# A long convolution and a linear attention in one kernel: start-up constants in 16 bits, nine warm-up matmuls, and another order of the units

## The chip, the cores and the metric

The kernel runs on one core of a Trainium2 chip. A core has five engines that each work through their own list of instructions in order: TensorE (PE, with its weight loads shown apart as PEld), VectorE (DVE), ScalarE (ACT), GpSimd (POOL) and SyncE (SP), which here issues all the DMA transfers. An instruction waits until the results and buffers it needs are there, and everything behind it on its engine waits with it. The metric is the time of one execution on the device in microseconds, median over repeated runs.

## The reference

Two independent computations on sequences of 2048 tokens with 576 features share one output, side by side. All inputs and outputs are bfloat16.

```python
# part A: causal short filter on k, product with v, long convolution by FFT, gate with q
k_shift = sum(k_pad[:, t:t + S, :] * shift_k[:, 3 - t] for t in range(4))
kv = k_shift * v
y = irfft(rfft(pad(kv)) * rfft(pad(ssm_k)))[:S] + kv * ssm_D
a = q * y
# part B: linear attention with 32 heads of 18, phi(t) = where(t > 0, t + 1, exp(t)) + 1e-6
q, k, v = split_heads(x @ wqkv)
pq, pk = phi(q), phi(k)
kv = einsum("bhsd,bhse->bhde", pk, v);  z = pk.sum(tokens)
o = einsum("bhqd,bhde->bhqe", pq, kv) / (einsum("bhqd,bhd->bhq", pq, z) + 1e-6)
b = o @ wo
out = concat([a, b], -1)
```

## The kernel before

The whole program is one list of some 295 units, the string `ORDER`. Each entry names a function of the kernel, its arguments, and behind the slash the buffer slots that it takes (four PSUM slots, and named rings in SBUF). The units are recorded in that order, so for every engine the list is also the order of its instructions; no scheduler moves anything. The digits behind the slash decide which earlier unit a new one has to wait for.

Part A works on five chunks `ci` of up to 128 features. The long convolution is a transform by matmuls in two steps of lengths 128 and 16. For the filter (`h`) and the signal (`u`) of each chunk, `h1`/`u1` multiply with the matrices G (128 positions by 128 frequencies for each of 16 residues, real and imaginary part, `s_ps`, L532), an eviction writes `Ch` or `Cu`, a transposing DMA (`ht`, `ut`, L539) makes `Cth` or `Ctu`, and `h2`/`u2` (L555) do the length-16 step into `T` and `SU`. The products `pX`, `pT`, `pS`, `pA` (L567 to L572) run on VectorE or GpSimd. `i1` (L589) and `i2` (L602 to L604) invert the transform; the last step multiplies with q in place, and `st` stores three groups of columns. `cv` (L487 to L493) is the short filter, on VectorE for the greater part, and needs k (`kl`), v (`vl`) and the shift weights `Wj`, which a matmul of ones with one row broadcasts over the partitions (`W_ps`, L387). `hd` and `hT` load D into the filter's first element and turn the filter to position-major by 16 TensorE transposes (L511).

Part B: `xl` loads four blocks of x, `xd` transposes them (L337, L342), `k`, `q` and `qt` are the projections (L451, L460, L468) with phi as an exponential on ACT (L443) and a max on VectorE (L444). `G` multiplies x with phi(k) (L659), `zs` sums phi(k) over the tokens, `kv` and `M` fold wv and wo into one matrix per head block, `den` makes the denominators and their reciprocals, `bc` and `bt` broadcast those and scale phi(q), and `o` and `ol` (L768 to L805) are the output matmuls, with their evictions into `ob` (L299 on ACT, L301 on VectorE) and their stores.

The start-up makes its constants itself. `io` and `ix` compute for each of 16 x 128 positions an integer phase modulo 8192: a float product, converted to 32-bit integers (L145), masked (L146), and for the cosine a quarter turn added and masked again (L150, L151), each in two halves `h`. `sin` turns the phases into G on ACT (L222). `wu` issues warm-up matmuls on zeros (L80), `dc` turns D into a column (`D_ps`, L430). The one row of shift weights lies in partition 96 of a tile whose other 96 rows are zeroed on ACT (`lz`, L377), so that `W_ps` multiplies 97 rows.

On SP, the load of the third filter chunk (`hl.2`) reuses a ring slot and waits for TensorE to have read the slot's content.

Of the kernel before, what the change touches and what calls it, by code (L numbers as in the profile page):

```python
# [8 lines left out]
FP32 = mybir.dt.float32  # L9
# [8 lines left out]
D = 576  # L18
# [19 lines left out]
k.15/3 u1.0.1.0.A/2 hT.2.D/21 u1.0.0.1.A/0 u1.0.0.0.A/3 ht.1.1/0 cv.1.1.DD xd.1.T/1 k.13/2 h2.1.1.1.A/11 cv.1.2.DD
h2.1.1.0.A/0 q.3.1/3 h2.0.0.1.A/21 h2.0.0.0.A/2 ut.0.0/0 cv.1.3.DDP hl.3/0 q.3.0/0 q.1.0/1 u2.0.0.0.A/03 k.6/2
ut.0.1/1 k.7/0 u2.0.0.1.A/3 pX.0.0.D/0 qt.1/1 u2.0.1.0.A/12 u2.0.1.1.D/0 k.5/3 u1.1.1.0.A/12 kl.1 pT.0.0.D k.12/1  # L40
pX.0.1.D/1 u1.1.0.1.A/0 k.14/2 u1.1.1.1.A/3 ht.1.0/0 ql.0/1 cv.2.0.D u1.1.0.0.A/0 pT.0.1.D k.4/1 cv.2.1.DD
h1.2.1.1.A/03 pS.0.1.D pA.0.0.P ut.1.1/1 h1.2.1.0.A/2 hd.3 pA.0.1.D q.1.1/0 h2.1.0.0.A/33 h2.1.0.1.A/2 G.1/10
# [31 lines left out]
def _warm(tc, psum, K, n):  # L74
# [4 lines left out]
    for _ in range({'A': 5, 'B': 8, 'C': 7, 'D': 6}[n]):  # L79
        nc.tensor.matmul(ps[:], lhsT=zero, rhs=zero.unsqueeze(1).to_broadcast([128, 4, 128]), start=True, stop=True)  # L80
# [163 lines left out]
def kernel(  # L244
# [71 lines left out]
    xT = {}  # L316
# [572 lines left out]
```

## Time and profile before

| what | value |
|---|---|
| median of 3 runs | 161.7 us (161.61 to 161.87) |
| span of the profiled execution, first to last instruction | 159.3 us |
| PE busy | 147.6 us, 1966 matmuls |
| VectorE busy | 139.8 us |
| ACT busy | 128.4 us |
| POOL busy | 65.2 us |
| DMA | 31.92 MB, 200 GB/s on average |

The page gives no other time of the profiled execution than its span; the median of the timed runs lies 2.4 us over it. In the profile's rows "L444 DVE ... out<-in ... x16 | 11.8, 751 | 2.7 <-ACT pk L443 2.6" means: line 444, on VectorE, 16 instructions, 11.8 us busy, 751 ns each, and 2.7 us of idle time before them, mostly ended by ACT. In the timeline a row begins with the start and the duration in us, and merges neighbours of one kind ("x16"); such a merged duration runs to the end of the last one. Matmuls overlap each other, so their count times the mean of one is more than the stretch they occupy; the chain of waits gives the stretches without that overlap. Some matmuls are missing from the records (1966 of 1982 weight loads).

### The profile page before, as it was taken

The numbers are of one execution on the slowest core, as the hardware profiler recorded it, in microseconds if no ns is written. First come the engines' busy times: TensorE is split into PE (matmuls) and PEld (weight loads), VectorE is DVE, ScalarE is ACT, GpSimd is POOL, SyncE is SP. The second block draws the span as 40 slices with busy tenths as digits, with TensorE's granted clock in tenths as the row PEclk, the third lists the DMA queues.
The fourth block names the chain that finished last, engine by engine and source line by source line (L and its number), as shares of the span: only waits on it lengthen the run. The fifth ranks groups of instructions, "written<-read, shape, count | busy, mean of one in ns | idle before, by whom it ended". The sixth has DMA issues, their size and how long they took to land.

```text
span 159.3 us, 4563 instructions
## 1 busy us (share of the span) xinstructions
PE 147.6 (93%) x1966; PEld 92.2 (58%) x1982; DVE 139.8 (88%) x170; ACT 128.4 (81%) x157; POOL 65.2 (41%) x67
## 2 busy tenths in 40 slices
PE   6799999999999999999998999999878999998990
PEld 1498564465734467467466568576445565677550
DVE  7978699899899999999899989998999999998420
ACT  7979996899997999959996956997999685786331
POOL 7407541806510970008100019589997077400000
PEclk9999999999999999999999999999999999999999
DMA  3999999990979999999999999684999999444282
GB/s 105 352 368 294 255 239 305 152 231 3 164 130 228 243 228 240 189 212 312 159 196 272 242 155 212 187 141 90 268 152 184 175 324 204 124 117 136 62 264 100
DMA packets 74171, 31.92 MB, mean 200 GB/s; under 512 B 52074, under 2 KB 73509, under 8 KB 74150
## 3 DMA queue, kind: packets, MB, share of 16 engines
q1 hardware_dynamic: 74150, 31.62, 91.7%
q8 instruction: 15, 0.25, 0.7%
q14 instruction: 6, 0.05, 0.1%
HBM read 14.97 MB, written 4.72 MB: 124 GB/s over the span
## 4 chain that ended last, share of the span: by engine, by line
PE 66%; POOL 12%; DVE 8%; DMA 6%; issue 3%; ACT 3%; SPq 0%; DVEq 0%; ACTq 0%; POOLq 0%
PE k_ps L451 12%; PE q_ps L460 11%; PE g_ps L659 6%; PE o_ps L776 6%; PE s_ps L532 6%; POOL X L567 5%; PE s_ps L555 5%; DMA Cth<-Ch 4%; PE i_ps L589 3%; POOL T L569 3%; PE hT_ps L511 2%; DMA pqT<-in_A_shift_k_dram 2%; PE xT_ps L337 2%; PE i_ps L602 2%; PE qt_ps L468 2%
## 5 line engine op out<-in xcount | busy, mean ns | idle before, releaser
L451 PE MATMUL k_ps<-wqk,xT 128*128 128x512 bf16 (+1 forms) x154 | 21.3, 282 | 0.3
L532 PEld LDWEIGHTS <-G 128*128 128x128 bf16 x320 | 17.4, 98 | 3.7 <-issue 3.4
L299 ACT ACTIVATE Cu<-s_ps 128x1024 bf16<-128x1024 f32 (+1 forms) x18 | 16.9, 978 | 2.1 <-DMA Cth<-Ch 1.4
L460 PE MATMUL q_ps<-xT,wqk 128*128 128x512 bf16 x78 | 18.2, 379 | 0.1
L451 PEld LDWEIGHTS <-xT 128*128 128x128 bf16 x160 | 11.4, 98 | 10.5 <-issue 0.5
L299 ACT ACTIVATE Ch<-s_ps 128x1024 bf16<-128x1024 f32 (+1 forms) x17 | 15.0, 928 | 3.0 <-PE s_ps L532 2.7
L299 ACT ACTIVATE ob<-o_ps 128x576 bf16<-128x576 f32 (+1 forms) x12 | 7.5, 636 | 11.3 <-PE o_ps L768 5.1
L299 ACT ACTIVATE V<-i_ps 128x1024 bf16<-128x1024 f32 x16 | 15.7, 1034 | 1.0 <-PE i_ps L589 1.0
L659 PE MATMUL g_ps<-pk,x_sb 128*128 128x65 bf16 (+1 forms) x124 | 16.3, 283 | 0.2
L299 ACT ACTIVATE T<-s_ps 128x1024 bf16<-128x1024 f32 x16 | 15.7, 1027 | 0.5 <-POOL at L490 0.5
L490 DVE TENSOR_TENSOR at<-at 128x2048 bf16<-128x2048 bf16 (+1 forms) x13 | 14.9, 1143 | 0.7 <-POOL at L489 0.3
L489 DVE TENSOR_TENSOR at<-k,Wj 128x2048 bf16<-128x2048 bf16 (+1 forms) x13 | 14.8, 1136 | 0.4 <-POOL at L490 0.4
L776 PE MATMUL o_ps<-wo_M,pqT 128*128 128x64 bf16 (+1 forms) x108 | 13.8, 283 | 0.5 <-issue 0.5
L444 DVE SCALAR_TENSOR_TENSOR pk<-pk,k_ps 128x576 bf16<-128x576 bf16 x16 | 11.8, 751 | 2.7 <-ACT pk L443 2.6
L299 ACT ACTIVATE SU<-s_ps 128x1024 bf16<-128x1024 f32 x14 | 14.1, 1029 | 0.0
L659 PEld LDWEIGHTS <-x_sb 128*128 128x128 bf16 x128 | 8.4, 97 | 8.7 <-issue 1.1
L460 PEld LDWEIGHTS <-wqk 128*128 128x128 bf16 x80 | 7.5, 98 | 9.1 <-issue 1.1
L443 ACT ACTIVATE pk<-k_ps,neg 128x576 bf16<-128x576 f32 x16 | 11.6, 745 | 1.2 <-PE k_ps L451 0.9
L604 DVE TENSOR_TENSOR q<-i_ps,q 128x1024 bf16<-128x1024 f32 (+1 forms) x10 | 11.0, 1107 | 1.2 <-PE i_ps L603 1.2
L776 PEld LDWEIGHTS <-pqT 128*128 128x128 bf16 x112 | 7.4, 98 | 7.6 <-issue 0.9
L490 POOL TENSOR_TENSOR at<-at 128x2048 bf16<-128x2048 bf16 (+1 forms) x2 | 6.2, 3097 | 12.9 <-DVE at L489 12.9
L532 PE MATMUL s_ps<-v,G 128*128 128x128 bf16 (+1 forms) x160 | 10.5, 214 | 1.0 <-ACT Cu L299 0.4
(161 smaller groups left out, 349.1 us busy)
## 6 DMA issues: line engine op xcount, KB each, us to landing
x_sb<-in_B_x_dram SPq DMA_DIRECT2D x4, 576.0 KB, 4.7
h_sb<-in_A_ssm_k_dram SPq DMA_DIRECT2D x4, 512.0 KB, 5.1
out_dram<-ob SPq DMA_DIRECT2D x7, 288.0 KB, 3.3
k<-in_A_k_dram SPq DMA_DIRECT2D x1, 1280.0 KB
v<-in_A_v_dram SPq DMA_DIRECT2D x1, 1280.0 KB, 8.5
q<-in_A_q_dram SPq DMA_DIRECT2D x1, 1280.0 KB
wqk<-in_B_wqkv_dram SPq DMA_DIRECT2D x2, 576.0 KB, 7.6
k<-in_A_k_dram SPq DMA_DIRECT2D x1, 1024.0 KB
```

What stands on the lines that cost most here:

```text
L299: nc.scalar.activation(out=out, in_=in_, func=ACT.Copy)
L443: nc.scalar.activation(out=out_ap, in_=ps_ap, func=ACT.Exp, bias=K.neg1[0:n, :])
L444: nc.vector.scalar_tensor_tensor(out=out_ap, in0=out_ap, scalar=1.0, in1=ps_ap, op0=ALU.min, op1=ALU.max)
L451: nc.tensor.matmul(ps[:, n0:n1], lhsT=xT[r // 4][:, t, rr * 128:(rr + 1) * 128], rhs=wqk[:, t, D + n0:D + n1], start=(t == 0), stop=(t == 4))
L460: nc.tensor.matmul(ps[:, j, :], lhsT=wqk[:, t, 128 * c:128 * c + 128], rhs=xT[g][:, t, :], start=(t == 0), stop=(t == 4))
L489: on[0].tensor_tensor(out=t_, in0=kk[:, 3 - stage:19 - stage], in1=wb(stage), op=ALU.mult)
L490: on[1].tensor_tensor(out=a_, in0=a_, in1=t_, op=ALU.add)
L532: nc.tensor.matmul(ps[:, bi, 0:dc], lhsT=K.G[ri][:, b, :], rhs=xf(b), start=True, stop=True)
L555: nc.tensor.matmul(ps[q:q + 32, z, :], lhsT=K.W0[64 * z:64 * z + 64, x, :], rhs=Ct[64 * z:64 * z + 64, r, :, j, :], start=True, stop=True)
L604: nc.vector.tensor_tensor(out=qs, in0=ps[:, :, 0:dc], in1=qs, op=ALU.mult)
L659: nc.tensor.matmul(ps[:, n0:n1], lhsT=x_sb[:, r, f0:f0 + fn], rhs=pk[:, r, n0:n1], start=(r == 0), stop=(r == 15))
L776: nc.tensor.matmul(pss[i][:, n0:n1], lhsT=pqT[:, c, r * 128:(r + 1) * 128], rhs=B['M'][:, c, n0:n1], start=(c == 0 and not first), stop=(c ...
```

## The change

Six things change.

- The phase index is built in 16-bit integers. The first residue comes from a float product over 128 columns, converted and masked; the other 15 by doubling: residues n to 2n are residues 0 to n plus n times the position constant, which GpSimd has written for the four powers of two. Masking with 8191 comes behind.
- The zeroed 96 rows are gone: the shift weights lie in partition 0, and `W_ps` multiplies one row. Its load is the first on SP.
- Warm-up matmuls: five, and four more in a second unit.
- The column sums that become the selection matrix `zsel` leave `kv` for a unit `zz` of their own, placed among the first inverse steps.
- The reciprocals lie in the tile of the token sums (`Gz`) instead of the tile of wo and M.
- The last output block is stored in the pieces in which it is evicted.

And the list of units is another one: positions, slots, and the engines of some products and evictions.

```diff
 ORDER = """
-io dl ix.0.0/0 hl.0/0 lz sin.1.0 eps ix.1.0/1 id ls ix.0.1 iw ix.1.1 xl.2 sin.0.0 wk wu.1.A/0 lw.2 dc/1 hd.0 Wj.A/230
+io ls ix.0.0/0 sin.1.0 wu.1.A/0 wu.2.B/1 dl ix.1.0/1 sin.0.0 hl.0/0 dc/2 hd.0 Wj.A/301 ix.0.1 id xl.2 iw ix.1.1 sin.0.1
...
-st.1 o.1.3.DAs/23 i2.3.0/1 i1.4.0.0.A/00 i1.4.0.1.A/3 i2.3.1/2 i2.4.1/1 i2.4.0/0 st.2 o.0.3.AAs/32 o.1.1.DA/10
-ol.0.1/320
...
+o.0.3.DAs/31 i2.4.0/0 i2.4.1/2 st.2 o.1.1.AA/31 ol.0.1/023
...
-    for _ in range({'A': 5, 'B': 8, 'C': 7, 'D': 6}[n]):
+    for _ in range({'A': 5, 'B': 4}[n]):
...
+    K.mul = K.sm[:, 1160:1416].bitcast(I16).rearrange("p (i k) -> p i k", i=4)
+    for i in range(4):
+        nc.gpsimd.iota(K.mul[:, i], pattern=[[4 << i, 128]], base=-(1 << i), channel_multiplier=0)
...
-        nc.vector.tensor_tensor(out=K.mp[:, b], in0=kap, in1=sv, op=ALU.mult)
-        nc.vector.tensor_single_scalar(out=K.mp[:, b], in_=K.mp[:, b], scalar=8191, op=ALU.bitwise_and)
+            m = slot([128, 2, 16, 128], I16, "mp")
+            K.ma, K.mp = m[:, 0], m[:, 1]
+        if h == 0:
+            first = K.sm[:, 840:968].bitcast(I32)
+            nc.vector.tensor_scalar(out=first, in0=K.sm[:, 128:256], scalar1=K.sm[:, 256:257], scalar2=None, op0=ALU.mult)
+            low = first.bitcast(I16).rearrange("p (k two) -> p k two", two=2)[:, :, 0]
+            nc.vector.tensor_single_scalar(out=K.ma[:, 0], in_=low, scalar=8191, op=ALU.bitwise_and)
+        for i in range(3) if h == 0 else (3,):
+            n = 1 << i
+            nc.vector.tensor_tensor(out=K.ma[:, n:2 * n], in0=K.ma[:, 0:n],
+                                    in1=K.mul[:, i].unsqueeze(1).to_broadcast([128, n, 128]), op=ALU.add)
+        nc.vector.tensor_single_scalar(out=K.mp[:, b], in_=K.ma[:, b], scalar=8191, op=ALU.bitwise_and)
...
-    K.Srow = pqT[0:97].rearrange("o c n -> o (c n)")[:, 0:4 * D]
+    K.Srow = pqT[0:1].rearrange("o c n -> o (c n)")[:, 0:4 * D]
...
-        nc.sync.dma_start(out=K.Srow[96:97, :], in_=A_shift_k.rearrange("(o d) j -> o (d j)", o=1))
-
-    def zero_rows():
-        z = K.sm[0:96, 1984:2048]
-        nc.scalar.activation(out=K.Srow[0:96, :].bitcast(FP32).rearrange("p (a b) -> p a b", b=64),
-                             in_=z.unsqueeze(1).to_broadcast([96, 18, 64]), func=ACT.Copy)
+        nc.vector.memset(K.sm[0:1, 769:833].bitcast(I32), 0x3F803F80)
+        nc.sync.dma_start(out=K.Srow, in_=A_shift_k.rearrange("(o d) j -> o (d j)", o=1))
...
-        B['rden'] = wm[:, 2 * n + 1152:2 * n + 1664]
...
+        gz = ring([128, 5, 512], BF, "Gz", "xT", 2)
+        B['Gz'] = gz[:, 0:2, :].rearrange("p a b -> p (a b)")[:, 0:D]
+        B['rden'] = gz[:, 2, :]
...
+
+    def b_zz():
+        B['zsel'] = ab.tile([128, 5, 32], BF, name="zsel")
         ps = psum.tile([128, 8], FP32, name="z_ps")
...
-            if n1 == 576:
-                nc.sync.dma_start(out=outB[:, r, D:2 * D], in_=B['ob'][:, r, 0:D])
+            nc.sync.dma_start(out=outB[:, r, D + n0:D + n1], in_=B['ob'][:, r, n0:n1])
```

The number of matmuls other than the warm-ups stays the same. Taken over the whole program, VectorE gives three full output evictions, two small evictions of transposed x, one of `SU` and one of `T` to ACT, and takes one of `V` from it; the other moves are between VectorE and GpSimd.

SP's list of transfers near the start of the program, before; `h_sb` is the filter, `wqk` the projection weights of part B, `k` part A's k with its halo rows, `x_sb` a block of x, and `Cth` the target of a transposing DMA:

```order
L361 DMA wqk<-in_B_wqkv_dram 128x4x576 x2
L404 DMA k<-in_A_k_dram 15x3x256
L406 DMA k<-in_A_k_dram 112x3x256
L409 DMA k<-in_A_k_dram 128x16x256
L438 DMA h_sb<-in_A_ssm_k_dram 128x2048
L539 DMA_TRANSPOSE Cth<-Ch 128x16x128
L319 DMA x_sb<-in_B_x_dram 128x4x576
```

The same place in the changed program:

```order
L442 DMA h_sb<-in_A_ssm_k_dram 128x2048
L370 DMA wqk<-in_B_wqkv_dram 128x4x576
L408 DMA k<-in_A_k_dram 15x3x256
L410 DMA k<-in_A_k_dram 112x3x256
L413 DMA k<-in_A_k_dram 128x16x256
L328 DMA x_sb<-in_B_x_dram 128x4x576
L543 DMA_TRANSPOSE Cth<-Ch 128x16x128 x2
```

The load of the third filter chunk has moved from behind k to a place ahead of the second half of the weights, of k and of the block of x; the first two transposes now follow each other.

VectorE's last instructions, before; `q` is the last result of part A, `ob` that of part B, `V` the half-inverted transform, `i_ps`, `o_ps` the matmuls' results:

```order
L301 CAST ob<-o_ps 128x576
L604 TENSOR_TENSOR q<-i_ps,q 128x8x128 x2
L604 TENSOR_TENSOR q<-i_ps,q 128x8x64 x2
L301 CAST ob<-o_ps 128x576
L301 CAST ob<-o_ps 128x288
```

And changed:

```order
L608 TENSOR_TENSOR q<-i_ps,q 128x8x128
L310 CAST V<-i_ps 128x8x32x4
L608 TENSOR_TENSOR q<-i_ps,q 128x8x128
L310 CAST ob<-o_ps 128x576
L608 TENSOR_TENSOR q<-i_ps,q 128x8x64 x2
L310 CAST ob<-o_ps 128x288
```

An eviction of `V` has come to VectorE, one of `ob` now stands between the products with q, and one `ob` at the end has left it.

More of the change, by code (lines that the diff above doesn't have):

```diff
@@ L38 @@
[L38 to L42, printed above, removed]
@@ L149, in _dft_index @@
             K.mc = slot([128, 2, 16, 128], I16, "mc")
-        nc.vector.tensor_single_scalar(out=K.mc[:, 0, b], in_=K.mp[:, b], scalar=6144, op=ALU.add)
+        nc.vector.tensor_single_scalar(out=K.mc[:, 0, b], in_=K.ma[:, b], scalar=6144, op=ALU.add)
         nc.vector.tensor_single_scalar(out=K.mc[:, 1, b], in_=K.mc[:, 0, b], scalar=8191, op=ALU.bitwise_and)
@@ L630, in load_wv @@
             nc.sync.dma_start(out=wg[h:h + 64, 0, 4, :], in_=wqkv[512:576, 2 * D:3 * D])
-        B['zsel'] = ab.tile([128, 5, 32], BF, name="zsel")
     def wo_M():
```

54 lines of the change are left out of this document (27 added, 27 removed).

## The prediction

> **What bounds the kernel now.** I read the page first, then the windows (busy time by stage), then the chain of waits in order of time, and the timeline of the two ends.
>
> ```profile
> PE 147.6 (93%) x1966; PEld 92.2 (58%) x1982; DVE 139.8 (88%) x170; ACT 128.4 (81%) x157; POOL 65.2 (41%) x67
> ```
>
> TensorE has 11.7 us without work in 159.3 us, VectorE 19.5 us. The stages say where (columns: busy us and instructions of PE, weight loads, DVE, ACT, POOL; then clock, DMA share, GB/s):
>
> ```profile
> 0.00:5.00 5.00, 2.53 (x10) 0.78 (x10) 3.80 (x13) 4.15 (x5) 3.87 (x24) 1.00 0.50 161
> 5.00:10.00 5.00, 4.85 (x33) 3.72 (x34) 3.95 (x9) 4.78 (x8) 0.82 (x1) 1.00 1.06 351
> 15.00:24.00 9.00, 8.89 (x85) 5.36 (x85) 7.04 (x12) 8.36 (x14) 4.45 (x16) 1.00 1.12 252
> ...
> 84.00:149.20 65.20, 60.66 (x1050) 41.02 (x1053) 62.34 (x73) 50.44 (x62) 33.36 (x12) 1.00 0.87 181
> ...
> 149.20:159.30 10.10, 6.37 (x54) 3.31 (x52) 1.22 (x2) 3.02 (x5) 0.00 (x0) 1.00 0.53 166
> ```
>
> Of PE's 11.7 idle us 2.6 lie before 10 us, 4.5 in 84 to 149.2 and 3.7 after that, which leaves 0.9 for 10 to 84 us: there PE sets the pace. From 84 to 149.2 us VectorE is the fuller one (2.9 us idle, PE 4.5). So removing work from either engine in the middle buys nothing by itself. Time can be had at the start, if the whole stream begins sooner, and at the end. The chain in order of time shows what the start consists of:
>
> ```profile
> 1.64 3.38 DMA pqT<-in_A_shift_k_dram
> ...
> 5.15 2.08 PE W_ps L387 x5
> 7.23 1.71 PE hT_ps L511 x16
> 8.94 1.52 PE xT_ps L337 x16
> ...
> 12.81 1.08 PE hT_ps L511 x16
> 13.88 0.89 PE xT_ps L337 x16
> ```
>
> The same sixteen transposes cost 1.71 and then 1.08 us, 1.52 and then 0.89 us. TensorE runs at about half pace until some point near 10 us, although the clock column prints 1.00 from the start; I go by the durations.
>
> **The change, part by part.** *The start.* PE now does nine warm-up matmuls instead of five.
>
> ```profile
> 1.06 2.31 PE L80 MATMUL warm_ps<-sm 128*128 128x512 bf16 x5 [1.06 <-DVE negpi L127]
> ...
> 3.31 0.29 PE L430 MATMUL D_ps<-sm 1*128 1x1 bf16 x5
> ```
>
> Nine at 2.31 / 5 = 0.46 us end at 1.06 + 4.16 = 5.2 us; the D matmuls take 0.29, so W_ps starts near 5.4 instead of 5.15: a loss of 0.3 us at most (0.1 if the five overlap as little as their last one suggests). The load of the shift weights, issued first instead of third, no longer decides: two places earlier, with the 3.38 us of its row, it lands before 5 us. What the warm-ups buy is that PE is busy from 1.06 us without the pause of 1.6 us before 5.15. Before, the full pace came between 3.8 us (8.94) and 5.3 us (10.46, end of the slow transposes) after the steady run began at 5.15. The same delay after 1.06 is 4.9 to 6.4 us, that is within W_ps. Then hT saves 1.71 - 1.08 = 0.63 us, xT 1.52 - 0.89 = 0.63, and W_ps 0 to 1.0 (half of 2.08). PE stands 1.0 to 2.2 us earlier behind them, bounds with the 0.1 to 0.3 us subtracted.
>
> The Trainium skill ("TensorE: Matmul & The Clock Gate", Part 1) says that about 3.4 us of sustained activity in a free-running window release the clock. By it the step falls between 4.5 and 7.9 us here, which is the same case as mine, with the late end half a microsecond dearer. Its Part 4 says that transposes do not count as activity; this trace disagrees, since the step came after some 3 us in which mostly transposes ran.
>
> Not all of that reaches the k matmuls. These rows are the hand-offs:
>
> ```profile
> 6.20 2.22 ACT L299 ACTIVATE Wj<-W_ps 128x1024 bf16<-128x1024 f32 x3 [0.18 <-PE W_ps L387]
> ...
> 8.97 1.23 DVE L301 COPY hT<-hT_ps 128x2048 bf16<-128x2048 bf16 x1 [0.91 <-PE hT_ps L511]
> ...
> 14.84 6.43 PE L451 MATMUL k_ps<-wqk,xT 128*128 128x512 bf16 x49
> ...
> 16.23 0.67 ACT L227 ACTIVATE sm<-sm,negpi 128x448 f32<-128x448 int32 x1 [0.20 <-DVE sm L198]
> ...
> 16.92 1.28 ACT L228 ACT_TABLE_LOAD   x1
> ...
> 18.32 2.62 ACT L443 ACTIVATE pk<-k_ps,neg 128x576 bf16<-128x576 f32 x4
> ```
>
> Worked through with the durations above: hT done near 7.9, its copy at 9.2, the first s_ps pair 9.2 to 10.1, the second hT to 11.1, second xT to 12.7, last s_ps 13.2, k_ps 13.5: 1.3 us before 14.84. ACT then has the last Ch at 15.0, the second sine 0.7, the table load 1.28: first exp near 17.15 instead of 18.32, 1.2 us sooner. The fifth k group waits for that exp's slot, so the stream is **1.2 us** earlier. If the clock is not released sooner, the same walk gives 0 to 0.3.
>
> *Sine index.* VectorE's four operations per half in 32 bits become 16-bit additions:
>
> ```profile
> L145 DVE TENSOR_TENSOR mp<-sm 128x1024 int32<-128x1024 f32 x2 | 2.4, 1192 | 0.2 <-POOL sm L122 0.2
> ...
> L146 DVE TENSOR_SCALAR mp<-mp 128x1024 int32<-128x1024 int32 x2 | 1.4, 694 | 0.1
> ...
> L151 DVE TENSOR_SCALAR mc<-mc 128x1024 int16<-128x1024 int16 x2 | 0.9, 426 | 0.1
> ...
> L120 POOL IOTA sm<- 128x128 f32 x1 | 0.2, 238 | 0.4 <-POOLq L873 0.4
> ```
>
> The masks fall from 0.69 to 0.43, the multiplications (2.4) become additions over 1,920 elements, no dearer than 1.2 per 1,024 and no cheaper than 0.43: 0.8 to 2.2. VectorE saves 0.8 to 2.4 us before 8 us, at a time when it waits for PE (the copy of hT waited 0.91). It is worth 0, and four more index operations on POOL, 0.24 each or less, fit in front of the additions. The zeroing of 96 rows on ACT ran beside this, before the first sine could start: 0 too.
>
> *Loads.* Here the change takes a risk. On SP, where a waiting instruction holds all behind it, the third h load, whose buffer PE must first have read, now stands ahead of the q weights, of k and of the first transposes (the first pair of lists above).
>
> ```profile
> 6.97 1.60 SPq L409 DMA_DIRECT2D k<-in_A_k_dram  x1
> ...
> 12.84 1.33 SPq L438 DMA_DIRECT2D h_sb<-in_A_ssm_k_dram  x1
> ...
> 14.54 5.75 SPq L539 DMA_TRANSPOSE Cth<-Ch  x1
> ...
> 23.54 1.23 DVE L487 TENSOR_TENSOR at<-k,Wj 128x2048 bf16<-128x2048 bf16 x1
> ...
> 30.95 0.62 PE L555 MATMUL s_ps<-Cth,W 64*32 64x512 bf16 x16
> ...
> k<-in_A_k_dram SPq DMA_DIRECT2D x1, 1024.0 KB
> ...
> h_sb<-in_A_ssm_k_dram SPq DMA_DIRECT2D x4, 512.0 KB, 5.1
> ```
>
> The second hT, its reader, is done near 11.1, so the h load goes out near 11.5, after 1.7 us or more its first bytes move (144 KB take that to land, in a row below), and k's main load is issued near 14 instead of 6.97. With it lie in front 0.5 MB of h, 0.6 of the weights (half the columns of wqk's upper four blocks, 576 KB) and 1.2 of k with its halo rows, at the 250 to 350 GB/s of the stages above 7 to 9 us: k lands at 20 to 23 us, wanted at 23.5 - 1.2 = 22.3. With 2 us for the x load and 2 to 3 for each of the two transposes (an estimate: the row's 5.75 holds the queue's backlog too) these land at 26 to 31, wanted at 30.95 - 1.2 = 29.8. Cost 0 to 1.3 us; I take **0.3**.
>
> *Middle.* The z matmuls and the selection matrix leave the kv unit and come 20 us earlier; the reciprocals lie in another tile. Same instructions, 0.3 us of VectorE among others: 0. Three of the four full output evictions move from VectorE to ACT, which has 14.8 us idle in 84 to 149.2; but VectorE takes other copies back, so from its first full-width conv on it has as much to do as before: 0, bounds ±1.0 for waits that the new order closes or opens (PE's 4.5 us there are many of 0.2 to 0.6).
>
> *The end.* The output unit o.0.3 now precedes the last two products, and one V eviction is on VectorE (the second pair of lists above).
>
> ```profile
> 145.22 1.94 ACT L299 ACTIVATE V<-i_ps 128x1024 bf16<-128x1024 f32 x2 [0.80 <-PE i_ps L589]
> ...
> 146.41 0.22 PE L603 MATMUL i_ps<-V,F 128*128 128x128 bf16 x1
> 147.21 0.19 PE L602 MATMUL i_ps<-V,F 128*128 128x64 bf16 x1 [0.59 <-ACT V L299]
> ...
> 148.81 3.87 PE o_ps L776 x31
> ...
> 149.19 0.58 SPq L824 DMA_DIRECT2D out_dram<-q  x1
> ...
> out_dram<-ob SPq DMA_DIRECT2D x7, 288.0 KB, 3.3
> ...
> out_dram<-ob SPq DMA_DIRECT2D x2, 144.0 KB, 1.7
> ```
>
> PE stood from 146.47 to 147.21 for V; o.0.3's 2.3 us (half of 3.87 and its head) cover it: **0.7** gained. If that cover failed, 0. The last store shrinks from 144 to 72 KB: by the slope 3.3 - 1.7 per 144 KB at most 0.8, at least 0; I take **0.2**. The last store of q moves to 149.19 + 2.3 - 0.7 = 150.8.
>
> Sum: -1.2 + 0.3 + 0 - 0.7 - 0.2 = **-1.8**. VectorE is the fuller engine after 84 us, and what PE gains at 147 us it can give back there, since o.0.3 adds an eviction of 0.7 us ahead of the last products. I give back 0.2 for that and keep -1.6: the profiled span goes from 159.3 to 157.7, and the median, which lies 2.4 us over that span, from 161.7 to **160.1 us**. Bounds: 158.6 (2.2 at the start, 0.7, 0.2) to 161.0 (0.3 at the start, losing 0.3 in the loads, 0.7 at the end).
>
> **The rivals.** (1) *The clock is not released sooner.* W_ps has one row now where it had 97, so its 2 us may not count as work, and the warm-ups alone may be too short. For it: five of them, 2.31 us, did not do it. Against: nine last 4.2 us. Then only the end is left: -0.7 to -1.0, 160.9. (2) *VectorE passes on nothing.* Its 62.34 of 65.20 us set the pace from 84 us, and its work is not less. Then the early start turns into waits in front of it: 161.7. Against it: its start also depends on PE's k groups, 1.2 us sooner. (3) *Slower: the h load at the head of SP's queue.* If the loads behind it run at 250 GB/s, k lands at 23 and the second transpose at 31 or, with x in front of it, 32: PE stands 1.2 to 2.2 us at the first s_ps of Cth, and VectorE begins its conv later than before. It decides once that landing is past 30.95. Slow clock with it: 162.7. (4) *The last q store ends the kernel.* Loads of 576 KB took 4.7 us and of 1024 KB 8.7, so 768 KB issued at 150.8 land at 155.5 to 159.5 against 157.7 for the last ob store before: up to +1.0 over the forecast, about 161.
>
> ```profile
> x_sb<-in_B_x_dram SPq DMA_DIRECT2D x4, 576.0 KB, 4.7
> ...
> v<-in_A_v_dram SPq DMA_DIRECT2D x1, 1024.0 KB, 8.7
> ```
>
> **How the numbers follow.** Forecast 0.47 (160.1), rival 1 0.17 (160.9), rival 4 0.05 (161), rival 2 0.14 (161.7), rival 3 0.17 (162.7). The measurement tells 0.2%, 0.3 us, from no change: faster is the first three, 0.69; same 0.14; slower 0.17. Range 158.6 to 162.4: from the gain bound to most of rival 3; the forecast's own range is 158.6 to 161.0.
>
> **What would show it.** Right: W_ps, hT and xT at the pace of the second hT and xT; the first exp near 17.2 us; the first s_ps of Cth near 29.8 with no wait on the transpose; no gap of PE ahead of the last i_ps; a last store of 72 KB. Wrong: hT at 1.7 us again; a wait on k or Cth between 20 and 32 us; PE gaps between 100 and 130 us grown by what the start gave; the q store landing last.

## The result

The changed kernel takes 158.62 us (median of 20 runs, 157.72 to 161.44), the kernel before on the same chip 161.19 us (20 runs, 160.24 to 162.97). The ratio is 0.9842, 95% interval 0.9818 to 0.9867: 1.6% faster, where the forecast was 1%. Ratios leave out executions that are counted as slow, of which the changed kernel has two among its 20 (without them its median is 158.48 us).

The profiled execution of the changed kernel has a span of 157.6 us (159.3 before). The busy times of its page, and its windows at the same stages as before, the last ones shifted by the 1.7 us that the span lost (columns: busy us and instructions of PE, weight loads, DVE, ACT, POOL; clock, DMA share, GB/s):

```profile
PE 149.6 (95%) x1986; PEld 90.3 (57%) x1986; DVE 135.8 (86%) x169; ACT 130.5 (83%) x162; POOL 62.0 (39%) x70
```

```profile
0.00:5.00 5.00, 3.94 (x16) 1.43 (x17) 3.51 (x16) 2.87 (x4) 2.44 (x21) 1.00 0.49 145
5.00:10.00 5.00, 4.55 (x60) 3.58 (x59) 4.20 (x11) 4.97 (x10) 0.12 (x1) 1.00 1.07 386
15.00:24.00 9.00, 9.00 (x83) 5.28 (x81) 6.82 (x11) 8.72 (x16) 3.62 (x15) 1.00 1.13 291
...
84.00:147.50 63.50, 61.47 (x1007) 38.99 (x1006) 59.35 (x69) 51.42 (x64) 29.32 (x11) 0.97 0.82 171
147.50:157.60 10.10, 6.56 (x80) 3.84 (x77) 2.34 (x4) 2.90 (x5) 0.00 (x0) 1.00 0.54 166
```

Between 5 and 10 us PE now issues 60 matmuls instead of 33. Between 84 us and the tail PE idles 2.0 us instead of 4.5, but there the clock column shows 0.97. The start in PE's timeline, two rows of ACT and VectorE, and SP's transfers:

```profile
1.06 3.65 PE L79 MATMUL warm_ps<-sm 128*128 128x512 bf16 x9 [1.06 <-DVE negpi L129]
4.64 0.27 PE L434 MATMUL D_ps<-sm 1*128 1x1 bf16 x5
4.78 1.13 PE L391 MATMUL W_ps<-pqT,sm 1*128 1x512 bf16 x5
5.92 1.16 PE L515 MATMUL hT_ps<-ident,h_sb 128*128 128x128 bf16 x16
7.16 1.05 PE L346 MATMUL xT_ps<-ident,x_sb 128*128 128x128 bf16 x16
...
12.96 0.81 PE L455 MATMUL k_ps<-wqk,xT 128*128 128x512 bf16 x3
```

```profile
16.40 0.73 ACT L447 ACTIVATE pk<-k_ps,neg 128x576 bf16<-128x576 f32 x1
```

```profile
21.84 0.75 DVE L448 SCALAR_TENSOR_TENSOR pk<-pk,k_ps 128x576 bf16<-128x576 bf16 x1 [0.92 <-ACT pk L447]
22.51 1.22 DVE L491 TENSOR_TENSOR at<-k,Wj 128x2048 bf16<-128x2048 bf16 x1
```

```profile
11.11 0.35 SPq L442 DMA_DIRECT2D h_sb<-in_A_ssm_k_dram  x1
...
13.89 0.64 SPq L413 DMA_DIRECT2D k<-in_A_k_dram  x1
...
18.42 8.34 SPq L543 DMA_TRANSPOSE Cth<-Ch  x2
...
27.44 2.47 SPq L413 DMA_DIRECT2D q<-in_A_q_dram  x1
```

W_ps takes 1.13 us instead of 2.08: the full clock is there before it. The trace's clock records say when: released at 4.20 us, before at 10.08. The k matmuls begin at 12.96 instead of 14.84, the first exp (the first ACT row above) at 16.40 instead of 18.32, that is 1.9 us sooner. The end, with the evictions of VectorE, the last stores and their sizes:

```profile
145.04 1.21 DVE L310 CAST V<-i_ps 128x1024 bf16<-128x1024 f32 x1
146.17 1.21 DVE L608 TENSOR_TENSOR q<-i_ps,q 128x1024 bf16<-128x1024 f32 x1
147.34 0.76 DVE L310 CAST ob<-o_ps 128x576 bf16<-128x576 f32 x1
148.78 1.29 DVE L608 TENSOR_TENSOR q<-i_ps,q 128x512 bf16<-128x512 f32 x2 [0.69 <-PE i_ps L607]
```

```profile
150.10 0.58 SPq L830 DMA_DIRECT2D out_dram<-q  x1
...
153.56 1.56 SPq L817 DMA_DIRECT2D out_dram<-ob  x3
```

```profile
out_dram<-q SPq DMA_DIRECT2D x1, 768.0 KB, 4.8
...
out_dram<-ob SPq DMA_DIRECT2D x2, 72.0 KB
```

PE's wait for V ahead of the last products is gone. The q store lands at 154.9 (150.10 plus 4.8), 2.7 us ahead of the end.

To see where the time went I cut each profiled execution at four instructions that all kernels have: the first exp, the last q matmul, the last product with the broadcast denominators (VectorE), the last o_ps matmul. The entries are lengths in us, worked out from the start times of those instructions:

| | to first exp | to last q | to last broadcast product | to last o_ps | to the end | span |
|---|---|---|---|---|---|---|
| before | 18.32 | 47.57 | 55.20 | 34.19 | 4.02 | 159.3 |
| changed | 16.40 | 48.53 | 55.71 | 33.12 | 3.83 | 157.6 |
| difference | -1.92 | +0.96 | +0.51 | -1.07 | -0.19 | -1.7 |

So the start gave 1.9 and lost half of it again before 65 us; the end gave 1.1; and something between 65 and 121 us took 0.5. The two losses have their rows. The first, PE's timeline:

```profile
42.01 0.62 PE L559 MATMUL s_ps<-Cth,W 64*32 64x512 bf16 x16 [0.34 <-DMA Cth<-Ch]
...
48.24 0.41 PE L559 MATMUL s_ps<-Ctu,W 64*32 64x512 bf16 x8 [0.52 <-DMA Ctu<-Cu]
```

The second is the clock: windows of the changed kernel around the place where the page's row of the clock has a 7:

```profile
113.43:116.84 3.41, 2.88 (x42) 1.43 (x41) 3.41 (x4) 3.41 (x6) 3.41 (x2) 1.00 0.96 209
116.84:120.25 3.41, 3.41 (x36) 1.29 (x36) 2.72 (x3) 2.34 (x5) 3.41 (x3) 0.50 0.98 185
120.25:123.66 3.41, 3.05 (x69) 2.18 (x62) 3.38 (x5) 3.41 (x4) 1.13 (x1) 1.00 0.87 60
```

For 3.41 us TensorE ran at half clock, and VectorE and PE lost 0.76 us by it: in another profile of the same kernel (e11) that has no such window the stretch takes 54.95 us and not 55.71. The kernel as such is therefore a little faster than this execution; twelve of its 20 executions have spans of 156.0 to 156.9 us. Why the clock fell there is not shown. PE had been busy for 2.88 of the 3.41 us before, but the kernel before had only 2.46 in 115.90 to 119.31 and kept the full clock.

### The profile page after: what moved, and what is told of

Its sections match the earlier page's. It is cut to its first block, busy times and chain, and to the rows that moved or that the text cites. A ratio compares the mean times of both kernels' runs of the same rounds, so it can differ in the third digit from the quotient of the medians.

```text
span 157.6 us, 4600 instructions
## 1 busy us (share of the span) xinstructions
PE 149.6 (95%) x1986; PEld 90.3 (57%) x1986; DVE 135.8 (86%) x169; ACT 130.5 (83%) x162; POOL 62.0 (39%) x70
## 4 chain that ended last, share of the span: by engine, by line
PE 77%; ACT 12%; DMA 3%; DVE 3%; issue 1%; POOL 1%; DVEq 0%; POOLq 0%; ACTq 0%
PE k_ps L455 12%; PE g_ps L661 10%; PE o_ps L783 9%; PE s_ps L536 8%; PE q_ps L464 8%; PE i_ps L593 6%; PE s_ps L559 5%; DMA Ctu<-Cu 3%; PE i_ps L606 3%; PE i_ps L607 2%; ACT V L308 2%; ACT T L308 2%; ACT Cu L308 2%; PE o_ps L775 2%; ACT G L231 2%; PE qt_ps L472 2%
## 5 line engine op out<-in xcount | busy, mean ns | idle before, releaser
L308 ACT ACTIVATE T<-s_ps 128x1024 bf16<-128x1024 f32 x17 | 16.8, 1026 | 0.6 <-PE s_ps L559 0.6
L308 ACT ACTIVATE ob<-o_ps 128x576 bf16<-128x576 f32 (+1 forms) x15 | 9.2, 637 | 9.1 <-PE o_ps L775 4.8
L661 PE MATMUL g_ps<-pk,x_sb 128*128 128x512 bf16 (+1 forms) x128 | 16.5, 286 | 0.0
L494 DVE TENSOR_TENSOR at<-at 128x2048 bf16<-128x2048 bf16 (+1 forms) x14 | 15.5, 1109 | 0.5
L308 ACT ACTIVATE SU<-s_ps 128x1024 bf16<-128x1024 f32 x15 | 15.0, 1040 | 1.0 <-PE s_ps L559 1.0
L308 ACT ACTIVATE V<-i_ps 128x1024 bf16<-128x1024 f32 x15 | 14.7, 1039 | 1.0 <-PE i_ps L593 1.0
L783 PE MATMUL o_ps<-wo_M,pqT 128*128 128x512 bf16 (+1 forms) x112 | 14.9, 286 | 0.0
L536 PE MATMUL s_ps<-hT,G 128*128 128x128 bf16 (+1 forms) x160 | 10.7, 216 | 1.0 <-ACT G L231 0.4
L593 PE MATMUL i_ps<-W,T 64*128 64x128 bf16 x160 | 11.3, 217 | 0.4 <-DVE pqT L753 0.4
```

The lines of the kernel that those rows point to most:

```text
L308: nc.scalar.activation(out=out, in_=in_, func=ACT.Copy)
L494: on[1].tensor_tensor(out=a_, in0=a_, in1=t_, op=ALU.add)
L536: nc.tensor.matmul(ps[:, bi, 0:dc], lhsT=K.G[ri][:, b, :], rhs=xf(b), start=True, stop=True)
L593: nc.tensor.matmul(ps[:, r, g, :], lhsT=s[key, hf][64 * r:64 * r + 64, z, x, 128 * g:128 * g + 128], rhs=K.W[64 * r:64 * r + 64, m, :], st ...
L661: nc.tensor.matmul(ps[:, n0:n1], lhsT=x_sb[:, r, f0:f0 + fn], rhs=pk[:, r, n0:n1], start=(r == 0), stop=(r == 15))
L783: nc.tensor.matmul(pss[i][:, n0:n1], lhsT=pqT[:, c, r * 128:(r + 1) * 128], rhs=B['M'][:, c, n0:n1], start=(c == 0 and not first), stop=(c ...
```

## The experiments

**Five warm-ups (e1).** The changed kernel without the second unit of four.

```diff
-io ls ix.0.0/0 sin.1.0 wu.1.A/0 wu.2.B/1 dl ...
+io ls ix.0.0/0 sin.1.0 wu.1.A/0 dl ...
```

> The changed kernel without the four added warm-up matmuls, all else as changed. Theory (the start is the clock: full pace from 4.2 us instead of 10.1): W_ps, hT and xT run at half pace again, the step comes between 8.5 and 10.5 us, k_ps starts at 14.0 to 14.8 instead of 12.96, and of the changed kernel's gain of 2.5 us some 1.0 to 1.8 go: ratio to before 0.991 to 0.995. Rival (the new order and the 16-bit index make the start early, the warm-ups are idle): k_ps at 13.2 or sooner, ratio 0.984 as with them.

159.05 us (4 runs), ratio to before 0.9878 [0.9815, 0.9942]; span of the profile 156.9. PE's timeline:

```profile
3.82 2.08 PE L391 MATMUL W_ps<-pqT,sm 1*128 1x512 bf16 x5
5.92 1.87 PE L515 MATMUL hT_ps<-ident,h_sb 128*128 128x128 bf16 x16
7.58 1.91 PE L346 MATMUL xT_ps<-ident,x_sb 128*128 128x128 bf16 x16
9.29 0.48 PE L351 MATMUL xT_ps<-ident,x_sb 128*128 128x128 bf16 x4
```

The slow pace is back (W_ps 2.08, hT 1.87; clock released at 9.48), but W_ps starts at 3.82 where it started at 5.15 before, and the first exp comes at 16.98. The last q matmuls start at 64.98, with nine warm-ups at 64.93. In this order the four warm-ups bring the start 0.6 us, and in these two profiles all of it is gone by 65 us. The k matmuls start at 13.62, and this and the ratio lie between what the theory and its rival named. The interval holds the changed kernel's 0.9842, so these four runs do not show that the four warm-ups bring anything to the time in this order.

**The kernel before with nine warm-ups (e2).** Nothing else changed; W_ps keeps its 97 rows.

```diff
-... sin.0.0 wk wu.1.A/0 lw.2 dc/1 ...
+... sin.0.0 wk wu.1.A/0 wu.2.E/0 lw.2 dc/1 ...
```

> The kernel before with four more warm-up matmuls behind its five, nothing else. Theory (clock): the step comes before 7 us, k_ps at 13.0 to 13.6 instead of 14.84; how much of these 1.5 us arrives at the end is what the run is for: 0.7 to 1.5 us, ratio 0.991 to 0.996, if the middle passes on at least half. Rival (VectorE sets the pace after 84 us and passes on nothing): ratio 0.998 to 1.001 with the early start visible. Rival (the order is needed for it): step early, k_ps no sooner than 14.3.

159.61 us (4 runs), ratio 0.9898 [0.9813, 0.9983]; span 157.9. Its timeline, and its waits of PE after 143 us:

```profile
1.06 4.24 PE L80 MATMUL warm_ps<-sm 128*128 128x512 bf16 x9 [1.06 <-DVE negpi L127]
...
5.45 1.22 PE L387 MATMUL W_ps<-pqT,sm 97*128 97x512 bf16 x5
6.50 1.15 PE L511 MATMUL hT_ps<-ident,h_sb 128*128 128x128 bf16 x16
```

```profile
PE i_ps L602 <- ACT V L299: 0.6, 1, 0.6
```

The first exp comes at 16.95, 1.37 us sooner, and the end 1.40 sooner. Between them the lengths are 47.68, 55.03, 34.15 and 4.09, all within 0.2 of the kernel before: in this profile the middle, VectorE included, passes on the whole of an early start. The V wait stays. So the clock alone is worth 1.4 us in the former order by the traces; the ratio's interval reaches from 0.3 to 3.0 us.

**q loaded later (e3, e7).** The changed kernel waits at 42 and 48 us behind q's load of 1 MB, so the load was moved behind `ht.1.0` (e3), and behind `hl.4`, the x load being ahead of it (e7).

```diff
-... cv.0.3.DDD h2.0.1.0.A/3 eps ql.0/1 q.2.0/1 ...
+... cv.0.3.DDD h2.0.1.0.A/3 eps q.2.0/1 ...
-... ht.1.0/1 xl.1 ... cv.2.0.D hl.4/1 pT.0.1.D ...
+... ht.1.0/1 ql.0/1 xl.1 ...                       (e3)
+... ht.1.0/1 xl.1 ... cv.2.0.D hl.4/1 ql.0/1 pT.0.1.D ...   (e7)
```

> The changed kernel with the first load of q moved back from ahead of the fourth h load to behind the transposes of the second chunk, some 25 us later. Theory (half of the 1.9 us won at the start is lost between 40 and 49 us, where PE waits 0.34 us for Cth and 0.52 for Ctu since 1 MB of q stands ahead of h, x and the transposes): both waits go, the last q_ps starts at 64.0 instead of 64.93, and 0.3 to 0.9 us arrive at the end: ratio 0.979 to 0.982. Rival (the waits come from the chain of evictions, or VectorE takes the gain back): last q_ps 0.2 us earlier at most, ratio 0.984.

> The changed kernel with the first load of q behind the last loads of x and of the filter, some 30 us later (the earlier try put it ahead of x, and the G matmuls then waited 1.5 us for x). Theory (q's 1 MB ahead of other loads costs PE its 0.9 us of waits at 42 and 48 us): waits gone, and no wait on x; PE's last q_ps 0.5 to 0.9 us sooner after the first exp than as changed (48.5 us); at the end 0.3 to 0.9 us. Rival (VectorE's pace after 84 us takes it back): the same end, ratio 0.984.

e3: 161.6 us (4 runs, 158.53 to 161.94; spans of 156.8 once and 159.9 to 160.2 three times, no ratio). e7: 160.27 us (10 runs), ratio 0.9879 [0.9839, 0.992]. PE's waits between 40 and 96 us, e3 first:

```profile
PE g_ps L661 <- DMA x_sb<-in_B_x_dram: 1.5, 1, 1.5
```

```profile
PE s_ps L536 <- DVE v L497: 0.6, 1, 0.6
PE s_ps L559 <- DMA Ctu<-Cu: 0.3, 1, 0.3
```

The stretch from exp to the last q shrinks to 47.5 in both (48.5 in the changed kernel), which is the length before. But in both profiles the clock came late, at 10.1 and 13.2 us with the same nine warm-ups (that is taken up under e11), and so did the exp, at 17.95 and 19.26. An exp that comes late shortens the stretch by itself, since the queue gets ahead of PE. The profile of e11, the changed kernel with the exp at 19.20, shows how much: q's load goes out only 1.5 us later than in the changed kernel's first profile (28.96 and 27.44), the exp comes 2.8 us later, and the stretch takes 47.8, with this one wait between 26 and 66 us:

```profile
PE s_ps L559 <- DMA Ctu<-Cu: 0.2, 1, 0.2
```

And e8 below, with q's load in its place and the clock early, takes 47.5 without a wait. So of the 1.0 us 0.2 to 0.3 are left for q's load (e7 and e3 against e11). It does stand in front of the transpose: SP is done with issuing that Cth at 36.0 us in e3 and e7, at 38.4 in the changed kernel and 39.5 in e11. That it is what cost the changed kernel its 0.9 us is not shown. What the runs show is that in this order the transposes come just in time: PE waits there for nothing in e8, for 0.2 us in e11, 0.9 in the changed kernel and 1.3 in e10, and the rest of the stretch is 47.5 to 47.7 in all of them.

Later, in e3 G waits 1.5 us for the block of x, in e7 PE waits for the products and a later transpose. The shortest spans of e7 lie at 157.4 to 157.7 where the changed kernel has 156.0 to 156.9; the one short span of e3 is 156.8. No gain shows from a later q load.

**The last units as before (e4, e5).** The changed kernel with the former tail: o.0.3 behind the products again, the last V on ACT. In e4 the slots were mine, in e5 the tail is the former one word for word.

```diff
-... i1.3.1.1.A/1 o.1.3.AAs/02 i2.3.0/3 i1.4.0.0.A/01 i1.4.0.1.D/0 i2.3.1/2
-o.0.3.DAs/31 i2.4.0/0 i2.4.1/2 st.2 o.1.1.AA/31 ol.0.1/023
+... i1.3.1.1.A/1 o.1.3.DAs/23 i2.3.0/1 i1.4.0.0.A/00 i1.4.0.1.A/3 i2.3.1/2 i2.4.1/1 i2.4.0/0
+st.2 o.0.3.AAs/32 o.1.1.DA/10 ol.0.1/320          (e5)
```

> The changed kernel with the end in the order of before: the last two products with q ahead of the output unit o.0.3, and the V and ob evictions on the engines of before. Theory (o.0.3 covers the wait for V, 0.7 us): PE stands 0.6 to 0.8 us ahead of the last products and the kernel is 0.5 to 0.8 us longer, ratio 0.988. Rival (the end hangs on the last output store alone, the wait only moves): within 0.2 us of the changed kernel, ratio 0.984.

> The changed kernel with its last twelve units exactly as before, slots and engines included (the earlier try of this put two units on one slot). Theory (o.0.3 covers the wait for V): PE stands about 0.7 us ahead of the last products, the stretch from the last full set of G matmuls to the end is 0.6 to 0.9 us longer than in the changed kernel, ratio to before 0.987 to 0.990. Rival (the end of the new order is worth more, since it also takes VectorE's evictions off PE's way): 1.2 us or more, ratio 0.992 or above. Rival (nothing): 0.984.

e4: 160.35 us (10 runs), ratio 0.9972 [0.9933, 1.0012], with waits of PE of 1.12 us at 144 and 0.71 us at 148 us that my choice of slots had made; it says nothing on the order. e5: 159.97 us (10 runs), ratio 0.9918 [0.9868, 0.9967], about 0.8% slower than the changed kernel and between the theory (up to 0.990) and its rival (from 0.992). From the last broadcast product to the last o_ps it takes 34.78 us against 33.12. Of these 1.66 us, 0.75 are the V wait and 0.70 a wait of o.1.3 for a slot at 139 us, which only this mixture of two orders has.

**97 rows in W_ps (e6).** The changed kernel with the former 97-row W_ps and the zeroing on ACT.

```diff
-io ls ix.0.0/0 ...
+io ls lz ix.0.0/0 ...
-    K.Srow = pqT[0:1].rearrange(...)
+    K.Srow = pqT[0:97].rearrange(...)
```

> The changed kernel with the shift weights broadcast from 97 rows again, 96 of them zeroed, nine warm-ups kept. Theory (matmuls of one row don't count as work for the clock, so the nine warm-ups end at 4.9 us too early for some positions of its window, and the step slips to 10 us as it did in one run of the changed kernel's code): with 97 rows the busy stretch runs on to 7 us, the step comes by 7.7 us in every execution, and spans of 157.8 us and more with a clock without a mid-kernel drop disappear; median 0.2 to 0.5 us below the changed kernel's. Rival (rows don't matter, the window's position alone does): the same spread of spans, median as changed.

158.28 us (6 runs, 158.16 to 158.57), ratio 0.9792 [0.9757, 0.9828]. All six spans lie between 156.4 and 156.9. Its median is the lowest of all versions, but the 0.3 us to the changed kernel's 158.62 are not clear of noise, and e8 reaches shorter spans. Its lengths are 16.37, 48.27, 54.95, 33.12 and 3.80: where the changed kernel's profile has 55.71 with the half-clock window, the middle at full clock takes 54.95, as in e11. The zeroing costs nothing (exp at 16.37).

**32-bit sine index (e8).** The changed kernel with the former index, edited as in the diff of the change, backwards.

> The changed kernel with the phase index in 32 bits again, its order and warm-ups kept. Theory (VectorE waits there anyway, worth 0): k_ps within 0.2 us of the changed kernel's for the same clock, ratio 0.984. Rival (the shorter index is needed once the clock is early, since G is on the way of the first s_ps): first s_ps and k_ps 0.4 to 1.0 us later, of which at most half arrives at the end.

158.59 us (4 runs), ratio 0.9808 [0.975, 0.9865]; span 156.1. The index does make the filter late, so that PE waits at the transposes:

```profile
6.63 1.19 PE L505 MATMUL hT_ps<-ident,h_sb 128*128 128x128 bf16 x16 [0.36 <-DVE sm L179]
```

The first exp comes at 16.70, 0.3 later, and the last q matmul at 64.21, 0.7 earlier than in the changed kernel: the waits at 42 and 48 us are absent, and SP is 1.0 us ahead (it issues v's load at 25.79 instead of 26.81). Why it is ahead is not shown. At the end no loss is left.

**Clock and tail alone (e9, e13).** The kernel before with nine warm-ups and the changed tail. In e9 the tail has the changed kernel's slot numbers, in e13 those which come free first in the former order.

```diff
-io dl ... wu.1.A/0 lw.2 dc/1 ...
+io dl ... wu.1.A/0 wu.2.E/0 lw.2 dc/1 ...
-st.1 o.1.3.DAs/23 i2.3.0/1 i1.4.0.0.A/00 i1.4.0.1.A/3 i2.3.1/2 i2.4.1/1 i2.4.0/0 st.2 o.0.3.AAs/32 o.1.1.DA/10
-ol.0.1/320
+st.1 o.1.3.AAs/02 i2.3.0/3 i1.4.0.0.A/01 i1.4.0.1.D/0 i2.3.1/2 o.0.3.DAs/31 i2.4.0/0 i2.4.1/2 ...    (e9)
+st.1 o.1.3.AAs/23 i2.3.0/1 i1.4.0.0.A/00 i1.4.0.1.D/2 i2.3.1/3 o.0.3.DAs/10 i2.4.0/2 i2.4.1/3 ...    (e13)
```

> The kernel before with two parts of the change and nothing else: four more warm-up matmuls (the 97-row W_ps stays) and the changed kernel's last units behind the third products (o.0.3 ahead of the last two i2). Theory: the clock (159.3 to 157.9 us of span with the warm-ups alone) and the end (changed 157.6 to 156.0 against 157.5 to 158.3 with the former last units) are the whole gain, so the span is 157.9 - 1.2 = 156.7 us, the time near 158.4 us, no stall of PE over 0.3 us ahead of the last i_ps. Rival: the rest of the changed order, the reciprocals and the column sums carry a part; then the span stays at 157.3 us or above and the time at 159.0 or above.

> As the run before nine warm-ups and the changed last units, but with the changed kernel's last units given the slots that come free first in the former order (there o.1.3 had taken the slot whose V eviction came last, and TensorE stood 1.77 us for it). Theory: clock and end are the whole gain; with the warm-ups alone the span was 157.9, from the last broadcast to the last output matmul it took 34.15 us against 33.12 in the changed kernel with 97 rows; so last o_ps at 119.7 + 33.1 = 152.8, span 156.7 to 156.9, time 158.4 us. Rival: the end only works behind the changed middle (the reciprocals, the column sums, the moved evictions); then the last o_ps lies at 153.5 or later and the time at 159.3 or above.

e9: 161.39 us (12 runs), ratio 0.9999 [0.9968, 1.0029]: the whole gain gone, in the profile through the slots of the tail. In the former order slot 0 is the last to be emptied, and o.1.3 now asked for it (PE's waits, 137 to 152 us):

```profile
PE o_ps L768 <- ACT V L299: 1.6, 1, 1.6
```

e13: 160.02 us (8 runs), ratio 0.9906 [0.9871, 0.9942]; span 157.7. The windows of e2 and then of e13 over the V wait:

```profile
140.00:146.00 6.00, 5.26 (x92) 4.01 (x90) 5.49 (x7) 4.11 (x5) 0.00 (x0) 1.00 0.51 136
```

```profile
140.00:146.00 6.00, 5.84 (x105) 4.27 (x100) 5.69 (x7) 4.23 (x6) 0.00 (x0) 1.00 0.52 141
```

The wait is gone, and from the last broadcast product to the last o_ps it takes 33.42 us against 34.15 in e2: 0.73 for the tail. But the time is the rival's: 0.9906 against the changed kernel's 0.9842, 1.0 us more. My theory that clock and tail are the whole gain falls. The profile of e13 has a rather late clock itself (7.11 us). Against e6 the e13 profile loses 1.02 before the first exp (17.39 against 16.37; in the former order with nine warm-ups and 97 rows the k matmuls start at 13.70, 13.90 and 14.06 in e2, e9 and e13, in the changed order at 12.96), regains 0.68 by the last q, and loses 0.21, 0.30 and 0.35 in the three stretches behind it. So by the times some 1 us of the gain belongs to the rest of the changed order, and no run takes that apart. The lower time of the tail does not show in e13's times against e2's either (spans 157.6 to 159.1 and 157.5 to 160.0); the stretch in the trace is the only evidence for its 0.73.

**The last block stored whole (e10).** e6 with the former store of 144 KB.

```diff
-            nc.sync.dma_start(out=outB[:, r, D + n0:D + n1], in_=B['ob'][:, r, n0:n1])
+            if n1 == 576:
+                nc.sync.dma_start(out=outB[:, r, D:2 * D], in_=B['ob'][:, r, 0:D])
```

> The changed kernel with 97 rows in W_ps, and the last block of ob stored whole (144 KB) as before. Theory: the time from the end of the last eviction by ACT to the end grows from 3.47 us by 0.1 to 0.3 us (before: 3.70), and the span with it, 156.6 to 156.8. Rival (pieces buy nothing, the store's fixed part is all): 3.4 to 3.5 us as now, 156.5.

158.70 us (4 runs), ratio 0.9828 [0.9785, 0.9872]; span 157.1. From the last o_ps to the end it takes 3.65 us, in e6 3.80. By these two profiles the rival is right: pieces buy nothing. The 0.6 us that its profile is behind e6 lie before 66 us.

**One row or 97 (e11, e12).** The changed kernel once more beside the others (e11), and the kernel before with nine warm-ups, one row in W_ps and no zeroing (e12).

```diff
-io dl ix.0.0/0 hl.0/0 lz sin.1.0 ... wu.1.A/0 lw.2 dc/1 ...                 (e12)
+io dl ix.0.0/0 hl.0/0 sin.1.0 ... wu.1.A/0 wu.2.E/0 lw.2 dc/1 ...
...
-    K.Srow = pqT[0:97].rearrange(...)
+    K.Srow = pqT[0:1].rearrange(...)
...
```

> The changed kernel itself, once more beside the others. Theory (with one row in W_ps the clock is released early in some executions and late in others): its spans scatter between 156.0 and 157.7 us, where 97 rows gave 156.4 to 156.9 six times; its time lies 0.2 to 0.6 us above that of the 97-row kernel (158.28). Rival (no difference by the rows): spans and time as with 97 rows.

> The kernel before with nine warm-ups and one row in W_ps, without the zeroing on ACT. Theory: matmuls of one row don't count as activity, so the clock is released late in some of the executions; spans lie in two groups, near 157.7 and at 159.0 or above, the median above the 159.6 us that the same kernel with 97 rows gave. Rival: the warm-ups alone are enough; all spans 157.5 to 158.0, time 159.6.

e11: 159.79 us (6 runs), spans 156.3, 156.9, 157.3 and three times 158.9 or 159.0, a wider spread than either expectation. The profile is one of the latter, and its timeline shows the slow pace in spite of nine warm-ups (released at 12.69 us):

```profile
1.06 4.02 PE L79 MATMUL warm_ps<-sm 128*128 128x512 bf16 x9 [1.06 <-DVE negpi L129]
5.02 0.29 PE L434 MATMUL D_ps<-sm 1*128 1x1 bf16 x5
5.17 2.08 PE L391 MATMUL W_ps<-pqT,sm 1*128 1x512 bf16 x5
7.18 1.07 PE L515 MATMUL hT_ps<-ident,h_sb 128*128 128x128 bf16 x8
```

The first exp is at 19.20. e12: 159.36 us (12 runs), ratio 0.9893 [0.9854, 0.9932], about what 97 rows gave there (159.61): the median of 159.6 or more that the theory wanted did not come. Seven of its spans lie at 157.0 to 157.7, one at 158.2, three at 159.2 to 159.3 with a mean clock of 0.97 to 0.98, and one at 159.9 with the clock undiminished once it was there, as in e11.

The clock records of all these profiles fit one picture. The stretches from the release to the next change last 109.23, 112.64, 146.77, 150.19 or 153.60 us, which are 32, 33, 43, 44 and 45 times 3.413, so the clock is decided on a grid of 3.413 us, and the grid lies differently in every execution. Counting back from the release gives the window that was judged, and those before it that failed. Windows that released: 0.79 to 4.20 (changed), 1.64 to 5.05 (e5), 2.42 to 5.83 (e12, the last 0.45 us of it one-row matmuls), 3.70 to 7.11 (e13, with W_ps of 97 rows). Windows that did not, though PE was busy without a pause: 2.45 to 5.86 (e11, 0.7 us of it W_ps with one row) and 5.86 to 9.28 (e11, 1.4 us of it), 3.28 to 6.70 (e3, 1.5 us), 2.99 to 6.41 (e7, 1.2 us) and 6.41 to 9.82 (e7, 0.8 us). The closest pair is e13 and e3: of their windows W_ps fills 1.67 and 1.53 us, with 97 rows in the one that released and with one row in the other (e13's row first, then e3's):

```profile
5.44 1.95 PE L387 MATMUL W_ps<-pqT,sm 97*128 97x512 bf16 x5
```

```profile
5.17 2.08 PE L391 MATMUL W_ps<-pqT,sm 1*128 1x512 bf16 x5
```

So matmuls of one row don't count as work, and a window may hold little of what doesn't: 0.45 us (e12) and 0.55 us (e3, 6.70 to 10.11) passed, 0.7 us did not. With 97 rows in W_ps almost nothing ahead of the transposes fails to count (the five D matmuls take 0.3 us): none of the ten executions of e6 and e10 is over 157.3 us, while 10 of 26 of the changed kernel are. That count is weaker than it looks, since not all ten need be late releases: the profiled one (157.6) was released at 4.20 us and is long by its half-clock window, and two more, at 159.7, have the same mean clock of 0.989. The windows carry the mechanism; e12's median says that a late release is seldom enough not to decide a median of the former order.

## Why the prediction was right or wrong

The direction was right, and so were the mechanisms of the early clock and of the covered wait for V; the size was not. 2.6 us were gained (161.19 to 158.62 in 20 runs each), 1.6 were forecast. The time itself lay 1.5 us under the forecast 160.1, since the starting value of 161.7, from three runs, was 0.5 high as well. The steps that failed are sizes: the start, the 0.2 given back at the end, and the middle, which was put at 0. By the lengths of e6, which differs in W_ps alone and whose profile has no half-clock window, the gain of 2.8 exceeds the forecast by 1.2: 0.35 from the start with the loads (1.25 for 0.9), 0.25 from the middle, 0.57 from the stretch to the last o_ps (1.07 for 0.5). The profiled execution's span of 157.6 meets the forecast 157.7 by luck, because 0.76 us were lost in its half-clock window. The terms:

- **The start, forecast -1.2, measured -1.92 at the first exp.** This step was mis-sized. Its bound of 2.2 held the value, and the release at 4.20 us came 0.7 ahead of the stretch that I gave it (4.9 to 6.4). So the last warm-ups were fast too, W_ps began at 4.78 where I had 5.4, and it took 1.13 us, as little as the working allowed. I had measured a delay from the start of steady work, 3.8 to 5.3 us, where the chip judges fixed windows of 3.41 us. The Trainium skill ("TensorE: Matmul & The Clock Gate", Part 1) describes such a free-running window and that the count of slow matmuls varies with its phase; the records agree, 3.413 us and releases at 4.2 to 7.1 us in the profiles in which it came early. In e2, where the order is the former one, the forecast is met: -1.37. What the working lacked is that the order moves the start without the clock: in e1, with five warm-ups and the release at 9.48, W_ps starts at 3.82 and the first exp comes 1.34 us sooner than before. So the four warm-ups bring 0.58 of the 1.92 in this order. And the 0 to 0.3 us for a clock that is not released sooner holds in neither case: it is 1.34 with five warm-ups, and with nine and a release at 12.69 (e11) the exp comes 0.88 later than before.
- **The loads, forecast +0.3.** Wrong in its place. The h load at the head of SP's queue cost nothing: h went out at 11.11 and k's main load at 13.89, as worked out, the conv at 22.51 waited only for ACT, and the first s_ps of Cth came at 29.04 without a wait. That refutes rival 3. The price came 12 to 18 us later, where I had not looked: 0.34 and 0.52 us at 42.0 and 48.2 us for transposes that stand behind q's load in the queue, and the stretch to the last q grew by 0.96. I had followed the queue past the first two transposes and not further. How much of the price is q's load stays open (e3, e7 and e11 leave 0.2 to 0.3 us for it); in the order as it is the price varies from 0 (e8) to 1.3 us (e10).
- **Start and loads together, forecast -0.9, measured -0.96 (64.93 against 65.89), -1.25 in e6.** That the sum fits in the profiled execution is luck: two errors cancel. e1, e6, e8 and e10 have their last q at 64.98, 64.64, 64.21 and 65.34 with exps at 16.98, 16.37, 16.70 and 16.40: how early the exp is does not decide it, the waits behind it do.
- **Sine index 0, zeroing 0.** The former holds at the end (e8), but not because VectorE had room: the 32-bit index delayed the hT by 0.36 us, and in that execution the waits at 42 and 48 us were absent. The latter holds by e6 (exp at 16.37).
- **The middle, forecast 0.** From the last q to the last broadcast product e6, e10 and e11 take 54.95 us against 55.20: -0.25. The profiled execution shows +0.51 for its half-clock window.
- **The end, forecast -0.7, less 0.2 given back.** From the last broadcast product to the last o_ps -1.07. Of this 0.73 is the V wait covered by o.0.3 (e13 against e2), which meets the term; nothing was given back, since VectorE kept up with the eviction that came ahead of the last products: it waits 0.69 for PE ahead of 148.78, and PE waits for nothing there. The step that failed is this give-back of 0.2; the other 0.3 lie between 120 and 140 us in the changed order and were not tried apart.
- **The last store, forecast -0.2.** From the last o_ps to the end -0.19 in the profile, but not through the pieces (e10: 3.65 whole, 3.80 in pieces). Which part of the change it is, or whether it only varies, stays open: 3.4 to 4.3 us occur.

The rivals: (1) named the right mechanism, one row that does not count, and gave it the wrong form. It does not keep the clock down always; the warm-ups release it where a window falls on them, and otherwise the clock comes at 10 to 13 us. (2) is refuted by the trace of e2, where the whole of 1.4 us arrives at the end. (4) did not occur, as q lands 2.7 us ahead of the end.

Added up from the profile of e6, 159.3 to 156.5: the start less what the loads took back 1.25, the covered wait for V 0.73, and 0.8 in small pieces of the changed order. These have a place (0.25 between the last q and the last broadcast product, 0.30 to the last o_ps, 0.2 at the end), but no run that isolates them, and neither the column sums' unit nor the reciprocals' tile was tried alone.

## What to carry to other kernels

To be released early in every execution, work has to cover a whole window of the clock wherever the window falls, that is two windows' length (6.8 us), and what follows the warm-ups has to count as work too: keep matmuls of one row out of that time, or widen them with zeros, which cost nothing here (e6). Whether that lowers the median is not shown. An early start does not bring the transfers forward: follow every one that the queue still holds to the place where it is wanted, not only the first. And compare only profiles whose clock came at the same time; a late one hides such waits. An order that is written out by hand cannot be moved in parts: the same tail with other slot numbers gave all of the warm-ups' gain back (e9), so undo a part with the slots of the order it stands in.

## What had not been expected of the hardware

- The clock is decided in windows of 3.413 us whose phase changes from execution to execution; the same nine warm-ups released it at 4.2 us or at 12.7 (e11), worth 2.8 us at the first exp and 1.3 in the span (158.9 against 157.6, though the early execution holds the half-clock window below).
- Matmuls of one row, which occupied PE for 2.08 us, counted as idle. Transposes count: e1 was released at 9.48 after a window from 6.06 on that holds nothing else, the kernel before at 10.08 after one that holds mostly transposes. The Trainium skill ("TensorE: Matmul & The Clock Gate", Part 4) says that transposes do not engage the full clock, and these records disagree.
- One window at half clock can come in the middle of the kernel (116.84 to 120.25, and 119.34 to 122.75 in e3), behind windows in which PE was busy for 2.88 of 3.41 us by the profile. What brings it on stays open: windows with 2.89 us (e7, from 115.63) and 2.46 us (before, from 115.90) were followed by the full clock. Between its last q and last broadcast product the changed kernel took 0.76 us more with it than without it (55.71 against 54.95 in e11).
